# Sixth product of five w_out stages split into seven small products of the next w_in stage

## The chip, the cores and the metric

One core of one Trainium2 chip runs the kernel alone. The metric is device time in microseconds (us) of one execution; lower is better. The engines are TensorE (PE, matmuls), VectorE (DVE), ScalarE (ACT), GpSimd (POOL) and SyncE (SP); PSUM takes the results of PE, and DVE and ACT move them out ("evict" them).

## What is computed

Softmax attention over 8 batches, 12 heads, 448 positions and 64 dimensions a head, and then a two-layer network over the 3584 tokens:

```python
scores = (1 / sqrt(64)) * q @ k.transpose(0, 1, 3, 2)
attn = softmax(scores)
x = (attn @ v).transpose(0, 2, 1, 3).reshape(3584, 768)
h = x @ w_in                        # 768 x 2048
y = maximum(0.01 * h, h) @ w_out    # 2048 x 768
```

## The kernel before, in words

**Two matrix products, each by seven.** Both products of the network are done in bf16 by Winograd's form of Strassen's scheme: a 2 x 2 block product takes seven block products, with sums of blocks made by DVE beforehand (`x_mix`, `w_in_mix`, `h_mix`, `w_mix`) and sums of results made as they leave PSUM.

**Stages.** The tokens are cut at 0, 640, 1152, 1664, 2176, 2688, 3072 and 3584 into seven stages. From stage 1 on, the kernel is a sequence hidden(1), second(1), hidden(2), ..., second(6). `hidden(i)` (L525 to 605) makes the leaky-ReLU layer of stage i, `second(i)` (L1140 on) its outputs. Attention for later stages is done in between: "bursts" of scores and exponentials (L322, L331) inside second, and "rows" (the product of the exponentials and v, L343 and L350, with a reciprocal and a multiplication by DVE, L978 and L979), in both. Where bursts and rows go is settled while the program is built, by a small planner (`place`) that holds a model of when each engine and slot comes free. The finished x is transposed into `xT` by DMAs that SP issues (L276), q and k into `qkT` likewise (L285). POOL loads q, k and v and casts them.

**PSUM.** Two banks, `g0` and `g1`, and three slots, `sc0` to `sc2`, of two banks each (a tile of 128 x 2 x 512 fp32).

**hidden.** Two rounds r (0, 1) of seven steps; in each step, two chains each do one product of six matmuls (L548), 256 columns wide in a stage of 512 tokens. The chain "g" alternates between g0 and g1, the chain "sc" between the first banks of two slots (sc2 and sc1; `chains`, `b` and `a`). In round 0 each step does sc first, then g; in round 1 g first. What evicts a product, by step: 0, an ACT copy (L560); 1, a DVE add (L563); 2 and 3, ACT copies (L568, L572); 4 and 5, DVE adds (L575, L578); 6, an ACT Prelu straight from PSUM. Further Prelus (L537) turn the sums into h. Rows stand behind steps 1 and 3 of round 1 in hidden(2) to hidden(5); hidden(6) has none.

**second.** Two `block_pair`s (c = 0, 1), each with two blocks of 128 tokens and outputs `o1` and `o2`. `early()` and `late()` do six products of eight matmuls of 384 columns (L682) on g0 and g1 in turn: first and second into o1's left half, third into its right half (`keep` copies, `join` adds; L687, L693), fourth into o2's right half, fifth into o2's left half and added to its right, and the sixth, on top of the fourth's bank, into o1's right half, which is then stored.

**The seventh product, already split.** Its two parts (c = 0 and 1) are not done in second but in the next hidden, together: as one product of 256 tokens x 1024 by 1024 x 384 that is split once more by Winograd's form into seven runs of four matmuls of 192 columns. `deep(i)` (L621 to 660) does one run (L645) behind each step from step 1 of round 0 on, in the two banks of slot sc0; each run is added to o2 by DVE (L649). Its sums of h are made by `deep_sums` (L621) and one more (L651), those of the weights by `mix_deep`. In stage 6 it is done inside second.

Of the kernel before, what the change touches and what calls it, by code (L numbers as in the profile page):

```python
# [16 lines left out]
def kernel(  # L17
# [9 lines left out]
    nc = tc.nc  # L27
# [21 lines left out]
    w_pool = ctx.enter_context(tc.tile_pool(name="weights", bufs=1))  # L49
    ld_pool = ctx.enter_context(tc.tile_pool(name="ld", bufs=2))  # L50
    cast_pool = ctx.enter_context(tc.tile_pool(name="cast", bufs=1))
    v_pool = ctx.enter_context(tc.tile_pool(name="vones", bufs=1))
# [5 lines left out]
    h_pool = ctx.enter_context(tc.tile_pool(name="h", bufs=1))  # L58
    o_pool = ctx.enter_context(tc.tile_pool(name="o", bufs=3))
    c_pool = ctx.enter_context(tc.tile_pool(name="c", bufs=5))  # L60
# [41 lines left out]

    NX = 12 * P

    def place_of(t):
        return (t - cuts[5]) % NX

    OVER = max(-t % S for t in cuts if place_of(t) == 0)
    xT_flat = xT_pool.tile([P, KD * NX + OVER], BF16, name="xT")
# [6 lines left out]
    QH, QW = MH // 2, NW // 2  # L116
    deep_mix = w_pool.tile([P, 3, QH, QW], BF16)
    KEEP = 4
    h = h_pool.tile([P, MD, (KEEP + 1) * P], BF16, name="h")
# [15 lines left out]
    for t in (w_in_mix, w_mix):  # L135
        t = t.rearrange("p x k n -> p (x k n)")
        for j in range(9):
            rooms.append(t[:, ts(j, 4 * NSC * D)])
    for _ in range(3):
        rooms.append(o_pool.tile([P, DM], F32, name="o").bitcast(BF16)[:, :4 * NSC * D])  # L140
    for j in range(2):
# [4 lines left out]
    def room(x, new):  # L146

        n = P if x and new else SC
        if not rooms:
            return ld_pool.tile([n, 2, NSC, D], F32, name="f" + "qkv"[x])  # L150
        return rooms.pop(0)[:n].bitcast(F32).rearrange("p (h so d) -> p h so d", h=2, so=NSC)
# [295 lines left out]

    def mix_deep():

        t, (t2, t3, t4) = w_mix[:, 2], (deep_mix[:, x] for x in range(3))  # L450
        lo, hi, left, right = slice(0, QH), slice(QH, MH), slice(0, QW), slice(QW, NW)
        sub, add = nc.vector.tensor_sub, nc.vector.tensor_add
        for by, o, x, y in (
            (sub, t3, t[:, hi, right], t[:, lo, right]),
            (add, t2, t3, t[:, lo, left]),
            (sub, t4, t[:, hi, left], t2),
            (sub, t[:, lo, right], t[:, lo, right], t[:, lo, left]),
        ):
            by(o, x, y)
            yield  # L460
# [19 lines left out]
    def close_ring(i):  # L480

        if place_of(cuts[i]) == 0 and cuts[i] % S:
            for hp in range(KD):
                nc.vector.tensor_copy(xT[:, hp, :OVER], xT_flat[:, (hp + 1) * NX:(hp + 1) * NX + OVER])
                yield
# [37 lines left out]
    def hidden(i):  # L523
# [9 lines left out]
        del slots[1:]  # L533
        chains = [banks, [x[:, 0] for x in taken]]

        def act(m, cols, x):
# [4 lines left out]
        def group(chain, m):  # L541
            b, a = (x[:, :2 * nh] for x in chain)
            left, right = slice(0, nh), slice(nh, n)
# [24 lines left out]
            nc.scalar.copy(c12, b)  # L568
            yield
            product(a, w_in_sb[:, near, ch], xT[:, near, two], first=True)  # L570
            c22 = fresh()
# [13 lines left out]

        ready = []
        more = deep(i - 1) if i > 1 else None
        for r in range(2):
            ms = [4 * r, 4 * r + 2]
            todo = [group(chains[x], ms[x]) for x in range(2)]  # L590
            for step in range(7):
                for y in range(2):
                    x = y if r else 1 - y
                    yield
                    if r == 0 and step == 2 and y:
                        nc.vector.tensor_sub(t4, xT[:, far, one], t2)
                    next(todo[x])
                    if i > 1 and (r or step) and y == 1:
                        next(more, None)
                    if step == 2 and ready:  # L600
                        mix_h(i, ready.pop(0))
            for c in chains:
                c.reverse()
            ready += ms
# [5 lines left out]

    def deep_sums(i):

        one, two = (ts(x[1], P) for x in spots(i)[1])
        lo, hi = slice(MH, MH + QH), slice(MH + QH, MD)
        s3, s1 = h_mix[:, :QH, 0], h_mix[:, QH:, 0]
        for by, o, x, y in (
# [6 lines left out]

    def deep(i):

        one, two = (ts(x[1], P) for x in spots(i)[1])
        lo, hi = slice(MH, MH + QH), slice(MH + QH, MD)
        s3, s1 = h_mix[:, :QH, 0], h_mix[:, QH:, 0]
        t, (t2, t3, t4) = w_mix[:, 2], (deep_mix[:, x] for x in range(3))
        left, right = slice(0, QW), slice(QW, NW)  # L630
        o = [kept[i, c] for c in range(2)]
        end = i + 1 == NR
        taken = [slots.pop(0) for _ in range(2 if end else 1)]
        b, a = (x[:, 0, :QW] for x in taken) if end else (taken[0][:, x, :QW] for x in range(2))
        for ps, first, x, w, c, cols in (
            (b, True, h[:, lo, one], t[:, :QH, left], 0, left),
# [3 lines left out]
            (b, False, s3, t3, 1, right),  # L640
            (a, False, h[:, hi, one], t[:, QH:, right], 0, right),
            (b, False, h[:, hi, two], t4, 1, left),
        ):
            for m in range(QH):
                nc.tensor.matmul(ps, x[:, m], w[:, m], start=(first and m == 0), stop=(m == QH - 1), skip_group_check=True)  # L645
            if end and c and (ps is a or cols is left):
                nc.scalar.copy(o[c][:, cols], ps)
            else:
                nc.vector.tensor_add(o[c][:, cols], o[c][:, cols], ps)  # L649
            if ps is a and first and c == 0:  # L650
                nc.vector.tensor_sub(h[:, hi, one], h[:, hi, one], s1)  # L651
            if ps is a and not first:
                store(o[0], token(i, spots(i)[1][0][1]), slice(0, NW) if end else slice(0, DM))
            if w is t4:
                if not end:
                    store(o[1], token(i, spots(i)[1][1][1]))
                slots.extend(taken)
            yield

    def block_pair(i, c):  # L660
# [10 lines left out]
        else:  # L671
            o1, o2 = (o_pool.tile([P, DM], F32, name="o") for _ in range(2))
        kept[i, c] = o2
        b, a = banks
# [20 lines left out]
        def early():  # L695
# [19 lines left out]
            yield from product(a, h[:, lo, two], t1, first=True)  # L715
            keep(o2, right, a, calm)
            yield

        def late():
            yield from product(b, s3, t3)  # L720
            if i:
                keep(o2, left, b, calm)
            join(o2, right, b)
            if i + 1 == NR:
                store(o2, t0, right)
            yield
            yield from product(a, h[:, hi, one], w_out_sb[:, hi, right])
            join(o1, right, a)
# [26 lines left out]
        if last:  # L755
            more = deep(i)
            for x, _ in enumerate(early()):
                if x == 0:
                    next(parts[0])
                yield  # L760
                if x % 2:
                    next(more)
                    yield
            for _ in more:
                yield
            yield from closing()
            return
        if not c:
            parts[:] = [deep_sums(i)]
        for x, _ in enumerate(early()):  # L770
# [3 lines left out]
        for x, _ in enumerate(late()):  # L774
            if i and not c and (x == 4 or x == 6 and i + 1 == NR):
                next(parts[0])
            yield
        if i:
            return
        yield  # L780
# [155 lines left out]
    def advance(calm=True):  # L936
        have = list(to["load"])
        for x in range(3 if calm else 0):
            u = to["load"][x]
            if u < NU and u - 3 < (to["cast"], to["cast"], to["v"])[x] and u - 4 < min(to["load"]):  # L940
                load_soft(u, 2, (x,))
                to["load"][x] += 2
# [84 lines left out]
    def fetch(n=3):  # L1027
        if to["q"] == NPE:
            return
        for x, y in enumerate(("q", "cast", "v")):  # L1030
            u = to["load"][x]
            if n and u <= ahead and (u <= FAR or u - 3 < to[y]):
                load_soft(u, 2, (x,))
# [104 lines left out]
    def second(i):  # L1138
# [5 lines left out]
        for c in range(len(spots(i)[1])):  # L1144
            for x, _ in enumerate(block_pair(i, c)):
# [6 lines left out]
                left -= place(i, left if i or c or x > 1 else 0, calm=x not in ((1, 2, 3) if i == 5 else (1, 2)), keen=need[min(i + 2, NR)], cap=NU if all(summed) else need[i + 2])  # L1152
                if c or x < 20 or not 0 < i < NR - 2:
                    turn_next(i)
                if i == 0 and not c:
# [21 lines left out]

    ins, outs, deeps = mix_w_in(), mix_weights(), mix_deep()
    early = [1, 2, 4, 6, 7, 9, 11]
# [28 lines left out]
    for i in range(1, NR):  # L1208
        if i == 1:
            await_x(need[i + 1] - 1)  # L1210
        for step, _ in enumerate(hidden(i)):
# [3 lines left out]
            if step % 4 == 2 and rows_done < nxt and (step > 16 or i == 1):  # L1215
                rows()
            turn_next(i)
        model.update(now=0.0, act=2.3, free={id(x): 0.9 if cuts[i + 1] - cuts[i] == 4 * P and i + 1 < NR else 1.2 for x in slots}, ready={})
        second(i)
# [30 lines left out]
```

## Time and profile before

| | |
|---|---|
| Median of 3 runs | 377.83 us (377.81 to 378.04) |
| Profiled execution | 377.8 us, of which the span of the profile is 376.0 |
| Granted PE clock | 1.0 |
| PE busy | 368.8 us, 4008 matmul rows |
| DVE, ACT, POOL busy | 255.9, 259.9, 190.6 us |
| hidden(2), hidden(3), hidden(4) | 22.66, 22.64, 22.65 us |
| hidden(5) (384 tokens), hidden(6) | 18.17, 20.65 us |
| second(1) to second(4) | 25.4 us each |
| second(5) | 23.57 us |

A page of the profile gives busy time by engine, the chain of work that ended last, and groups of instructions by line. The timeline gives single rows: start in us from the span's start, length, engine, line, operation and tile, how many instructions it sums up, and in brackets how long the engine was idle before it and what released it. A stage begins where its first matmul begins.

### The profile page before, as it was taken

The page shows a single profiled execution, that of the slowest core. Times are in us where ns is not written, and L with a number is a line of the kernel's source. Part 1 is how long each engine was busy: PE and PEld are TensorE (multiplying, and loading weights), DVE is VectorE, ACT ScalarE, POOL GpSimd, SP SyncE. Part 2 cuts the span into 40 slices and gives each one's busy share as a digit, 9 for nine tenths or more (in the row PEclk, how much of TensorE's full clock was granted, in tenths as well). Part 3 has the DMA queues.
Part 4 walks back from the last instruction along what each step waited for, and adds up shares of the span by engine and source line. Part 5 has one row for each costly group of instructions (what it writes and reads, how often), then busy time and mean ns, then how long its engine had stood idle before and what let it go on. Part 6 is the DMA issues. An engine that isn't in the chain of part 4 may idle for free.

```text
span 376.0 us, 10120 instructions
## 1 busy us (share of the span) xinstructions
PE 368.8 (98%) x4008; PEld 265.3 (71%) x4008; DVE 255.9 (68%) x559; ACT 259.9 (69%) x399; POOL 190.6 (51%) x376
## 2 busy tenths in 40 slices
PE   7999999999999999999999999999999999999996
PEld 3665658756698566996569966699665995679765
DVE  4764868767666967676686665875747775685763
ACT  6998895866768785758766587666787668636721
POOL 8985871996269979634588335692346020000000
PEclk9999999999999999999999999999999999999999
DMA  9999999999499876963969648999445740321123
GB/s 155 200 203 207 175 203 202 166 165 168 92 186 150 113 149 89 204 154 55 162 120 150 138 65 80 166 145 180 63 66 108 131 110 0 80 57 45 41 65 105
DMA packets 99600, 48.08 MB, mean 128 GB/s; under 512 B 64608, under 2 KB 96352, under 8 KB 99552
## 3 DMA queue, kind: packets, MB, share of 16 engines
q0 software_dynamic: 39600, 22.47, 45.6%
q1 hardware_dynamic: 59504, 24.50, 32.5%
q8 instruction: 31, 0.51, 0.6%
q10 hardware_dynamic: 448, 0.47, 0.4%
q14 instruction: 17, 0.14, 0.1%
HBM read 45.61 MB, written 11.01 MB: 151 GB/s over the span
## 4 chain that ended last, share of the span: by engine, by line
PE 95%; DMA 2%; DVE 1%; POOL 1%; ACT 1%; issue 0%; POOLq 0%; ACTq 0%
PE g L682 30%; PE g L548 14%; PE sc L548 14%; PE sc L322 7%; PE sc L350 6%; PE g L424 4%; PE sc L319 4%; PE sc L645 4%; PE sc L362 3%; PE g L820 2%; PE sc L343 2%; DMA w_in_mix<-in_v_dram 2%; PE g L362 1%; PE g L301 1%; PE sc L424 1%; POOL w_in_mix L163 1%
## 5 line engine op out<-in xcount | busy, mean ns | idle before, releaser
L331 ACT ACTIVATE e<-sc 128x896 bf16<-128x896 f32 (+1 forms) x144 | 123.6, 921 | 29.9 <-PE sc L322 20.4
L682 PE MATMUL g<-w_out_sb,h 128*128 128x384 bf16 (+1 forms) x440 | 84.1, 325 | 0.0
L682 PEld LDWEIGHTS <-h 128*128 128x128 bf16 x592 | 54.4, 98 | 41.2 <-issue 11.0
L537 ACT ACTIVATE h<-c 128x512 bf16<-128x512 f32 (+1 forms) x72 | 43.1, 610 | 30.2 <-DVE c L563 12.4
L548 PEld LDWEIGHTS <-w_in_sb 128*128 128x128 bf16 x576 | 54.6, 98 | 5.7
L190 POOL COPY qkb<-fq 112x512 bf16<-112x512 bf16 x34 | 22.6, 666 | 43.8 <-DMA qkT<-qkb 34.7
L548 PEld LDWEIGHTS <-w_in_mix 128*128 128x128 bf16 x432 | 40.5, 98 | 3.7
L201 POOL COPY v<-fv 128x384 bf16<-128x384 bf16 x30 | 17.7, 591 | 42.7 <-PE sc L350 40.2
L687 DVE COPY o<-g 128x384 f32<-128x384 f32 x47 | 26.0, 553 | 13.2 <-PE g L682 13.0
L350 PE MATMUL sc<-v,e 128*128 128x65 bf16 x720 | 33.3, 193 | 0.0
L322 PE MATMUL sc<-qkT 64*128 64x448 bf16 (+1 forms) x210 | 32.8, 352 | 0.0
L978 DVE RECIPROCAL rec<-sc 112x8 f32<-112x8 f32 x42 | 8.7, 207 | 34.7 <-PE sc L350 19.4
L350 PEld LDWEIGHTS <-e 128*128 128x128 bf16 x720 | 31.1, 98 | 1.3
L979 DVE TENSOR_TENSOR x<-sc,rec 112x512 bf16<-112x512 f32 x42 | 29.0, 691 | 1.6 <-DVE rec L978 0.2
L548 PE MATMUL g<-xT,w_in_sb 128*128 128x256 bf16 (+1 forms) x216 | 28.5, 268 | 0.0
L548 PE MATMUL sc<-xT,w_in_sb 128*128 128x256 bf16 (+1 forms) x216 | 28.5, 268 | 0.0
L693 DVE TENSOR_TENSOR o<-o,g 128x384 f32<-128x384 f32 x39 | 21.4, 550 | 9.0 <-PE g L682 4.4
L343 PE MATMUL sc<-v,e 128*128 128x130 bf16 x120 | 26.5, 221 | 0.0
L649 DVE TENSOR_TENSOR o<-o,sc 128x192 f32<-128x192 f32 x39 | 13.7, 351 | 18.3 <-PE sc L645 18.3
L682 PE MATMUL g<-w_mix,h 128*128 128x384 bf16 x128 | 24.6, 326 | 0.0
L163 POOL DMA_DIRECT2D fv<-in_v_dram x32 | 20.1, 641 | 7.8 <-DMA fq<-in_q_dram 2.9
L682 PE MATMUL g<-w_mix,hmix 128*128 128x384 bf16 x112 | 21.7, 326 | 0.0
(149 smaller groups left out, 742.4 us busy)
## 6 DMA issues: line engine op xcount, KB each, us to landing
fq<-in_q_dram POOLq DMA_DIRECT2D x17, 224.0 KB, 6.1
w_out_sb<-in_moe_w_out_dram POOLq DMA_DIRECT2D x4, 768.0 KB, 13.2
out_dram<-o SPq DMA_DIRECT2D x7, 336.0 KB, 3.3
w_in_sb<-in_moe_w_in_dram POOLq DMA_DIRECT2D x2, 1152.0 KB, 13.6
out_dram<-o SPq DMA_DIRECT2D x7, 288.0 KB, 3.1
fk<-in_k_dram POOLq DMA_DIRECT2D x15, 128.0 KB, 6.0
fv<-in_v_dram POOLq DMA_DIRECT2D x15, 128.0 KB, 5.1
out_dram<-o SPq DMA_DIRECT2D x7, 240.0 KB, 3.1
```

The costliest lines, as they stand in the source:

```text
L163: nc.gpsimd.dma_start(out=t[p, :n, :, :so].rearrange("p u h so d -> p (u h) (so d)"), in_=(q, k, v)[x][b, hs, keys].rearrange("h (p so) d ...
L190: by(t[:SC, x].rearrange("p so h d -> p h so d"), f)
L322: nc.tensor.matmul(ps[:, j, :S].rearrange("p (so s) -> p so s", so=NSC), t[p, 1, c], t[p, 0, :, :SC], start=True, stop=True,)
L331: nc.scalar.activation(e[:, :, c, :], ps[:n, :, :S], AX.Exp, scale=scale)
L343: nc.tensor.matmul(ps, e[:, EM + qc * SC:EM + qc * SC + P], vt[:, 2 * KC:].rearrange("p j d -> p (j d)"), start=True, stop=False, skip_gro ...
L350: nc.tensor.matmul(ps[:, j * (D + 1):(j + 1) * (D + 1)], e[:, at:at + P], vt[:, j * KC + c], start=False, stop=(c == KC - 1), skip_group_c ...
L537: nc.scalar.activation(hs[:, m:m + 2, cols], x.rearrange("p (m t) -> p m t", m=2), AX.Prelu, alpha=0.01)
L548: nc.tensor.matmul(ps[:, j * nh:(j + 1) * nh], w[:, kk, ts(j, P)], x[:, kk], start=(first and j == 0 and kk == 0), stop=(kk == KH - 1), sk ...
L682: nc.tensor.matmul(ps[:, cols], x[:, m], w[:, m], start=(first and m == 0), stop=(m == MH - 1), skip_group_check=True,)
L687: by(o[:, at], ps[:, :NW])
L693: nc.vector.tensor_add(o[:, at], o[:, at], ps[:, :NW])
L979: nc.vector.tensor_mul(x, ps[:, :, :, :D], rec.to_broadcast([SC, 2, 2 * NP, D]))
```

## The change

For stages 1 to 5 (`twice(i)`), second no longer does the sixth product. `deep(i, side, b, a)` now does either split product: side 1 is the seventh ("more"), side 0 the sixth ("also"). In hidden(i + 1), runs of the sixth are issued behind the first product of the steps (0, 3), (0, 4), (0, 6), (1, 0), (1, 1), (1, 3) and (1, 4) (round, step). They take the two banks of sc1, one of the two slots of the sc chain; that chain, from step 3 of round 0 on, alternates between the two banks of sc2. The seventh keeps sc0.

With it come: the fourth product is joined to o1 as well at once, in `early()`; the copy of o2's left half goes to ACT in the second pair (`idle`); four weight sums for the sixth (`mix_deep(0)`, into `deep_mix6` and, in place, a quarter of `w_out_sb`), made in hidden(1); since stage 6 still does its sixth product whole, POOL reloads that quarter of w_out after hidden(6). The o pool has four buffers, v's loads a pool of their own with one buffer, and the ring `xT` nine blocks of 128 tokens where it had twelve, with more small copies where a stage wraps (`close_ring`).

The core of the diff:

```diff
-    NX = 12 * P
+    NX = 9 * P
...
+    deep_mix6 = w_pool.tile([P, 3, QH, QW], BF16)
...
+    def deep_w(side):
+        t, d = (w_mix[:, 2], deep_mix) if side else (w_out_sb[:, MH:, NW:], deep_mix6)
+        return t, [d[:, x] for x in range(3)]
+    def twice(i):
+        return 0 < i < NR - 1
...
         chains = [banks, [x[:, 0] for x in taken]]
+        more, also, over = (iter(()) for _ in range(3))
+        if i > 1:
+            third = slots[0]
+            more = deep(i - 1, 1, *(third[:, x, :QW] for x in range(2)))
+            also = deep(i - 1, 0, *(taken[1][:, x, :QW] for x in range(2)))
+            chains[1].append(taken[0][:, 1])
+        else:
+            over = mix_deep(0)
...
-            b, a = (x[:, :2 * nh] for x in chain)
+            b, a, *then = (x[:, :2 * nh] for x in chain)
...
             nc.scalar.copy(c12, b)
             yield
+            for a in then:
+                pass
             product(a, w_in_sb[:, near, ch], xT[:, near, two], first=True)
...
+                    if i > 1 and (r, step, y) == (0, 1, 1):
+                        for _ in deep_sums(i - 1, 0):
+                            pass
+                    if not y and (r, step) in ((0, 3), (0, 4), (0, 6), (1, 0), (1, 1), (1, 3), (1, 4)):
+                        next(also, None)
...
             for c in chains:
-                c.reverse()
+                if len(c) == 3:
+                    c[:] = [c[2], c[0]]
+                else:
+                    c.reverse()
...
+            at = slice(cols.start + (0 if side else NW), cols.stop + (0 if side else NW))
+            for y in (c, 0) if ps is a and c and not side else (c,):
+                if end and c and (ps is a or cols is left):
+                    nc.scalar.copy(o[c][:, at], ps)
+                else:
+                    nc.vector.tensor_add(o[y][:, at], o[y][:, at], ps)
...
             keep(o2, right, a, calm)
+            if twice(i):
+                join(o1, right, a)
             yield
...
             if i:
-                keep(o2, left, b, calm)
+                keep(o2, left, b, idle if c and twice(i) else calm)
             join(o2, right, b)
...
+            if twice(i):
+                return
             yield from product(a, h[:, hi, one], w_out_sb[:, hi, right])
             join(o1, right, a)
             store(o1, token(i, x1))
...
+        if i + 1 == NR:
+            raw_q = (slice(None), slice(MH, MH + QH), slice(NW + QW, DM))
+            nc.gpsimd.dma_start(out=w_out_sb[raw_q], in_=w_out_v[raw_q])
```

## The prediction on record

> **What bounds the kernel now.** I read the page first: busy shares, then the chain that ended last.
>
> ```profile
> PE 368.8 (98%) x4008; PEld 265.3 (71%) x4008; DVE 255.9 (68%) x559; ACT 259.9 (69%) x399; POOL 190.6 (51%) x376
> PE 95%; DMA 2%; DVE 1%; POOL 1%; ACT 1%; issue 0%; POOLq 0%; ACTq 0%
> ```
>
> TensorE (PE) is busy 98% of the span, and 95% of the chain that sets the end is PE. The table of stretches says the same by stage: in hidden(2) (147.58 to 170.24 us) PE is busy 22.66 of 22.66 us, at a granted clock of 1.00, and so in all stages but the last. So a stage is as long as its matmuls, and two things alone move the time: matmul time taken out or put in, and waits that PE does not have today.
>
> Then the timeline, for the price of a matmul: the end of second(1) and the start of hidden(2), PE rows (start, length, then engine, line and tile; a row's length contains the drain of its last matmul, so prices are taken from start to start).
>
> ```profile
> 146.28 1.46 PE L682 MATMUL g<-w_out_sb,h 128*128 128x384 bf16 x8
> 147.58 0.82 PE L548 MATMUL sc<-xT,w_in_sb 128*128 128x256 bf16 x6
> ...
> 149.54 0.82 PE L548 MATMUL g<-xT,w_in_sb 128*128 128x256 bf16 x6
> ...
> 150.20 0.49 PE L645 MATMUL sc<-w_mix,h 128*128 128x192 bf16 x4
> ...
> 150.53 0.82 PE L548 MATMUL sc<-x_mix,w_in_mix 128*128 128x256 bf16 x6
> ```
>
> Eight 384-column matmuls take 147.58 - 146.28 = 1.30 us; six of 256 columns 150.20 - 149.54 = 0.66; four of 192 columns 150.53 - 150.20 = 0.33 (four such runs follow each other at 0.328).
>
> Last, how long a PSUM result takes to be evicted, since the change gives one chain of hidden less PSUM. VectorE (DVE) and ScalarE (ACT) rows of hidden(2):
>
> ```profile
> 149.81 0.69 DVE L563 TENSOR_TENSOR c<-c,sc 128x512 f32<-128x512 f32 x1 [0.62 <-PE sc L548]
> ...
> 163.34 0.82 PE L548 MATMUL sc<-x_mix,w_in_mix 128*128 128x256 bf16 x6
> 163.99 0.82 PE L548 MATMUL g<-xT,w_in_sb 128*128 128x256 bf16 x6
> ...
> 164.07 0.63 ACT L537 ACTIVATE h<-c 128x512 bf16<-128x512 f32 x1
> 164.60 0.58 ACT L568 COPY c<-sc 128x512 f32<-128x512 f32 x1
> ```
>
> The first: DVE was idle and took the sc product that PE left at 149.54 (PE's next row starts there) 0.27 us later, for 0.69 us. With 0.06 from a DVE end to the PE row that waited for it (15.59 to 15.65, qkT at the start of the run) a DVE eviction is 0.27 + 0.69 + 0.06 = **1.02 us** after PE finishes. An ACT copy that finds ACT free takes 0.20 (151.18 to 151.38) + 0.59 + 0.05 = **0.84**. The last two rows: the sc product that ended at 163.99 was copied only from 164.60 to 165.18, since a Prelu stood ahead on ACT; that eviction took **1.24** with its return. None of these costs anything today, because each sc product lands in the slot that the product before it did not use.
>
> **The change, part by part.**
>
> *Matmuls.* In stages 1 to 5, two pairs each lose the 8 matmuls of the sixth product: 16 x 0.1625 = 2.60 us. The next hidden gains 7 runs of 4 matmuls: 7 x 0.328 = 2.30. Net -0.30 a stage, -1.5 us over five, all on PE and so all on the path.
>
> *PSUM.* This is where I see the price. The seven new runs need a slot. They take sc1, one of the two that hidden's sc chain alternated between; the seventh product keeps sc0. From step 3 of round 0 on, the sc chain therefore alternates between the two banks of one slot, sc2. In the kernel as built, dependences go by slot: each sc product from there on waits for the eviction of the sc product just before it, though that lies in the other bank. (In the kernel before, the second run of the seventh product, L645, already waits so for the L649 add of the first.) The cover is what PE has between two sc products: the g product (0.66), each deep run between (0.33), attention rows (1.02 in the row spacing 161.68 to 162.68). Step by step, for hidden(2) to (5):
> - round 0, steps 3, 4, 5: cover 0.98, 1.31, 1.31 against 0.84 (ACT), 0.84 (ACT), 1.02 (DVE): nothing.
> - round 0, step 6: 0.98 against 1.02: 0.04.
> - round 1, steps 1, 2, 4: cover 1.31, 1.67 and 2.0 (rows): nothing.
> - round 1, step 3: 0.98 (g and one run) against the queued copy's 1.24: 0.26; nothing if ACT is free.
> - round 1, step 5: only a g product, 0.66, against 1.02 for step 4's L575 add: 0.36. The add for g goes first on DVE; adds follow each other at 0.60 (167.95 to 168.55), so it may be 0.43.
> - round 1, step 6: 0.66 against 1.02 again: 0.36.
>
> Queued behind the waiting matmul is everything on PE, since PE works in order; DVE, ACT and the next second() wait for PE. So these go on the path whole.
>
> *Start of hidden.* The second run of the seventh product waits, as it does now, for the add of the first. Today that add ends at 151.42 and the run starts at 151.84: 0.36 to spare after 0.06 of return. The change loads DVE ahead of it: second() is 2.60 shorter but its last exps stay as long; `keep(o2, left)` goes to ACT behind them; the join of o2's other half reads the same bank and so follows that copy. Today ACT ends the last exp 1.34 before hidden starts (146.24 to 147.58); with a run of 8 less (1.30) it would end at about hidden's start, the copy 0.84 to 1.33 after it, the join (0.55) and the x sums (0.3 each) after that. I get the first run's add 0.86 later than today, the stall 0.86 - 0.36 = 0.5. Bounds: 0 and 0.5; I take 0.45, since each link is a row of today's trace.
>
> Sum of waits for one hidden: 0.45 + 0.04 + 0.26 + 0.40 + 0.36 = 1.5. hidden(5) has 192-column products (0.49 each; its add takes 0.55), cover and eviction shrink alike. hidden(6) has no rows: step 2 of round 1 loses cover (0.66 against 1.02: 0.36), and its start has a shorter queue (0.3): again 1.5. Five stages: **+7.5 us**.
>
> *Elsewhere.* Seven more adds of 192 columns (0.35) and four h sums (0.42) put about 4 us on DVE in a hidden where it is busy 15.7 of 22.7; they go where PE runs deep runs, and the adds above are priced with that order. At nothing I cost: the join of o1 (moved, not added); four `mix_deep(0)` sums in hidden(1) and twelve more ring copies in the second() before stages 2, 4 and 6 (0.3 to 0.5 each; second() leaves DVE 22 to 36% idle, by the stretches); the stores of o1 (SP, one hidden later; the qkT transposes behind them on SP are needed 5 us later or more); v loads in one buffer (the v casts that PE's rows need are done four rows, about 15 us, ahead); the raw quarter of w_out reloaded by POOL after hidden(6): 196 KB, issued when the sixth new run is done, needed about 10 us later; 224 KB loads land in 6.1 us by the page's DMA rows, so 4 us to spare, and if that cover is gone the stage waits up to 3 (the 768 KB load's 13.2 us). The xT transposes of a stage's last rows land 2.3 to 4.3 us from issue, and second() now ends 2.60 earlier: 0 to 0.3 us in a stage, taken as 0. Bursts move against DVE's x: 0 to 0.1 a stage, taken as 0.
>
> *Sum.* -1.5 + 7.5 = +6.0; I take off 0.3 because the step 3 and step 6 terms are partly nothing when ACT is early: **+5.7 us**. The profiled execution took 377.8 us (span 376.0 and 1.8 around it), the median of the runs is 377.83, so the two agree and the forecast is 377.8 + 5.7 = **383.5 us**.
>
> **Rivals.**
>
> *A. No new waits: faster.* If the two banks of a slot were free of each other, only the product two steps back would have to be evicted, more than 2 us earlier, and all terms but the one at hidden's start vanish: 377.8 - 1.5 = 376.3 (376.8 with a few tenths a stage left). It decides at round 1, step 5: an eviction under 0.66 us ends the stall, and the shortest in the trace is 0.84. For it: the trace of before shows no PE wait of this kind, as the one such pair (L645) has 0.36 to spare. Against: the waits as built. The Trainium skill (PSUM — Partial Sum Buffer, section "PSUM bank collisions raise a hardware error") asks for guards by bank and quadrant; a program so guarded would have no wait between the two banks, and the time would be A's 376.3. No run here shows that, and the waits of this kernel are coarser. Chance 0.12.
>
> *B. Only the two bare gaps.* The stalls at steps 5 and 6 of round 1 (0.36 + 0.40) are certain if waits go by slot; the queue effects (start of hidden, step 3) may be hidden, as ACT's order shifts once PE stalls. Then 5 x 0.76 + 0.36 = 4.2, less 1.5: 380.5. Chance 0.24 (379.3 to 381.5).
>
> *C. More than this.* DVE, at (15.7 + 4)/24 = 82% in hidden, falls behind after the first stall, or xT lands late: 0.5 a stage more, 386 and above. Chance 0.08.
>
> *Forecast*, waits as listed, 381.5 to 386: chance 0.53. The remaining 0.03 is small waits that eat the gain, about 377.8.
>
> **How the numbers follow.** Range 379.3 to 387.0: it holds forecast and B whole and the lower half of C (0.53 + 0.24 + 0.04 = 0.81); A is left out. Differences under 0.2% (0.75 us) are about what cannot be told from no change here. Faster: A, 0.12. Same: 0.03. Slower: the rest, 0.85.
>
> **What would show it.** PE in the changed trace should have idle time in front of sc rows of the product line (L548, now L578) at steps 5 and 6 of round 1, some 0.4 us each, released by DVE's add of the step before; a like gap before the second run of the seventh product, released by DVE; PE matmul time over the run should be 1.5 us less. second() of stages 1 to 5 should be 2.6 us shorter and hidden(2) to (6) about 3.8 longer (2.30 + 1.5). Wrong it would be if those rows follow each other without a gap (A), if the gap at hidden's start is missing (B), or if the wait in front of PE is released by a DMA or POOL.

## The result and the profile after

The changed kernel takes **390.2 us** (median of 6 runs, 389.64 to 391.70) where the kernel before takes 378.02 (6 runs): a ratio of 1.033, 95% interval 1.0309 to 1.0351, or 12.2 us more. The forecast was slower by 5.7 us, in a range up to 387.0. The sign was right, the size forecast was half of what came. The profiled execution took 389.64 us, with a span of 387.9 (before: 377.8 and 376.0).

The page of the changed kernel, the busy shares and the chain:

```profile
PE 372.2 (96%) x4068; PEld 269.3 (69%) x4068; DVE 273.5 (71%) x630; ACT 262.0 (68%) x404; POOL 190.5 (49%) x377
...
PE 79%; DVE 8%; DMA 5%; ACT 3%; issue 3%; POOL 1%; DVEq 0%; ACTq 0%; POOLq 0%
```

PE's share of the chain fell from 95% to 79%: DVE, DMA and ACT now set pieces of the end. The waits of PE, longest sums first (what PE waited to do, for what; us in total, times, longest):

```profile
PE sc L578 <- DMA xT<-x: 4.2, 2, 3.2
...
PE sc L578 <- DVE c L607: 1.2, 5, 0.4
...
PE sc L697 <- DVE o L703: 0.6, 3, 0.2
PE g L578 <- DVE o L746: 0.3, 1, 0.3
...
PE sc L578 <- DVE c L593: 0.2, 1, 0.2
```

The rows for DVE are waits of the kind that was forecast; the fourth (the second g product of hidden(5)) was not on the list. The first row was forecast at nothing. (These times start where PE could have gone on; the gap in the timeline, start to start less the price of the matmuls, is about 0.17 us longer each, and gaps are used below.)

By stage, start to start from the PE rows of the timelines: second(1) to (5) went from 125.28 to 112.75 us, -12.53 (forecast: 5 x 2.60 = -13.0). hidden(2) to (6) went from 106.79 to 130.47, +23.68: 11.48 for the seven runs of five stages (5 x 7 x 0.328, as forecast), and **12.2 us of waits** where 7.5 were forecast. The start (0.41) and second(6) (0.27) make up the rest of the 11.8 us by which the span grew.

**Two kinds of wait.** hidden(2) shows the kind that was forecast. PE rows of its round 1, steps 4 to 6, and the DVE rows that they wait for:

```profile
168.41 0.82 PE L578 MATMUL sc<-x_mix,w_in_mix 128*128 128x256 bf16 x6
169.07 0.82 PE L578 MATMUL g<-xT,w_in_mix 128*128 128x256 bf16 x6
170.08 0.81 PE L578 MATMUL sc<-xT,w_in_mix 128*128 128x256 bf16 x6 [0.19 <-DVE c L607]
170.73 0.82 PE L578 MATMUL g<-x_mix,w_in_sb 128*128 128x256 bf16 x6
171.67 0.82 PE L578 MATMUL sc<-x_mix,w_in_sb 128*128 128x256 bf16 x6
```

```profile
169.34 0.69 DVE L607 TENSOR_TENSOR c<-c,sc 128x512 f32<-128x512 f32 x1
169.94 0.68 DVE L610 TENSOR_TENSOR c<-c,g 128x512 f32<-128x512 f32 x1
170.93 0.69 DVE L610 TENSOR_TENSOR c<-c,sc 128x512 f32<-128x512 f32 x1 [0.31 <-PE sc L578]
```

The sc product of 168.41 ends for PE at 169.07; DVE adds it from 169.34 to 170.03, and the next sc product starts at 170.08, though a g product alone would have let it start at 169.72. The gap is 0.35, the next one (170.73 + 0.66 to 171.67) 0.28.

hidden(4) shows the other kind. PE rows, then the chain of work there (start, length, what), then the POOL rows:

```profile
246.41 0.38 PE L578 MATMUL sc<-xT,w_in_sb 128*128 128x256 bf16 x2
249.99 0.60 PE L578 MATMUL sc<-xT,w_in_sb 128*128 128x256 bf16 x4 [3.19 <-DMA xT<-x]
```

```profile
241.86 0.70 DVE x L1042
242.56 0.02 issue
242.57 7.37 DMA xT<-x
249.94 0.04 issue
249.99 0.60 PE sc L578 x4
```

```profile
241.35 1.23 POOL L175 DMA_DIRECT2D fv<-in_v_dram  x2
242.56 0.73 POOL L175 DMA_DIRECT2D fq<-in_q_dram  x1
243.25 1.26 POOL L175 DMA_DIRECT2D fk<-in_k_dram  x2
```

The last x of stage 4 is done at 242.56 and its transpose is issued at once, but lands 7.37 us later; PE stands still in the second sc product of hidden. POOL issued the next loads of v from 241.35 on, and q and k right behind, so 672 KB of loads were in front of the transpose or beside it; those of v were issued 1.2 us ahead of it. In the kernel before, POOL reached the like loads at 247.58, 3.8 us into hidden(4):

```profile
247.58 1.24 POOL L163 DMA_DIRECT2D fv<-in_v_dram  x2
248.79 0.73 POOL L163 DMA_DIRECT2D fq<-in_q_dram  x1
249.49 1.26 POOL L163 DMA_DIRECT2D fk<-in_k_dram  x2
```

### The profile page after: what moved, and what is told of

The parts are those of the page before. It is cut to its first block, busy times and chain, and to the rows that moved or that the text cites. A ratio compares the mean times of both kernels' runs of the same rounds, so it can differ in the third digit from the quotient of the medians.

```text
span 387.9 us, 10326 instructions
## 1 busy us (share of the span) xinstructions
PE 372.2 (96%) x4068; PEld 269.3 (69%) x4068; DVE 273.5 (71%) x630; ACT 262.0 (68%) x404; POOL 190.5 (49%) x377
## 4 chain that ended last, share of the span: by engine, by line
PE 79%; DVE 8%; DMA 5%; ACT 3%; issue 3%; POOL 1%; DVEq 0%; ACTq 0%; POOLq 0%
PE g L735 23%; PE sc L578 11%; PE g L578 9%; PE sc L334 6%; PE sc L362 6%; PE sc L697 6%; PE g L436 4%; PE sc L331 4%; DMA xT<-x 3%; PE sc L374 3%; PE g L883 2%; PE sc L355 2%; DMA w_in_mix<-in_v_dram 2%; DVE c L607 2%; PE g L374 1%
## 5 line engine op out<-in xcount | busy, mean ns | idle before, releaser
L735 PEld LDWEIGHTS <-h 128*128 128x128 bf16 x512 | 46.7, 98 | 35.9 <-issue 11.0
L735 PE MATMUL g<-w_out_sb,h 128*128 128x384 bf16 (+1 forms) x360 | 68.4, 325 | 0.0
L578 PEld LDWEIGHTS <-w_in_sb 128*128 128x128 bf16 x576 | 54.5, 98 | 12.8 <-issue 7.4
L202 POOL COPY qkb<-fq 112x512 bf16<-112x512 bf16 x34 | 24.3, 716 | 55.3 <-DMA qkT<-qkb 41.5
L213 POOL COPY v<-fv 128x384 bf16<-128x384 bf16 x30 | 16.6, 555 | 41.9 <-PE sc L362 26.7
L703 DVE TENSOR_TENSOR o<-o,sc 128x192 f32<-128x192 f32 x79 | 26.9, 348 | 10.2 <-PE sc L697 10.1
L740 DVE COPY o<-g 128x384 f32<-128x384 f32 x42 | 23.2, 553 | 13.1 <-PE g L735 11.2
L374 PEld LDWEIGHTS <-e 112*128 112x128 bf16 x432 | 20.1, 98 | 2.2 <-issue 0.8
```

Of the source, the lines that this page charges most:

```text
L202: by(t[:SC, x].rearrange("p so h d -> p h so d"), f)
L374: nc.tensor.matmul(ps[:, qc, :], t[:SC, at:at + P], vt[:, c], start=(c == 0), stop=(c == NSC - 1),)
L578: nc.tensor.matmul(ps[:, j * nh:(j + 1) * nh], w[:, kk, ts(j, P)], x[:, kk], start=(first and j == 0 and kk == 0), stop=(kk == KH - 1), sk ...
L703: nc.vector.tensor_add(o[y][:, at], o[y][:, at], ps)
L735: nc.tensor.matmul(ps[:, cols], x[:, m], w[:, m], start=(first and m == 0), stop=(m == MH - 1), skip_group_check=True,)
```

## The experiments

Two theories stood at the start. W: the sc chain waits by slot, as forecast. L: POOL's loads, moved ahead of the transposes, make xT late. Rivals: S, xT is late because second() ends 2.6 us sooner after the last x, whatever POOL does; D, the waits in hidden are VectorE's lack of room and not the slots.

### e1: POOL waits for xT

```diff
-        if i == 1:
+        if i + 1 < NR:
             await_x(need[i + 1] - 1)
```

> The changed kernel with one edit: ahead of each of hidden(1) to hidden(5), not of hidden(1) alone, POOL waits until the xT of that stage's last row has landed, so its next loads of q, k and v are issued behind that transpose. Theory L (loads first in the DMA engines make xT late): PE's waits for xT at the start of hidden(3) and (4), 4.2 us in the changed kernel's trace, go, and waits of about 0.36 us for the seventh product's second run come back in their place; 390.2 becomes about 386.5. Rival S (xT is late because second() ends 2.6 us sooner after the last row): the waits stay, within 1 us of 390.2. Rival P (POOL late then hurts its casts, and bursts wait for qkT): above 390.2.

Measured: **384.75 us** (ratio to before 1.0175, 1.0146 to 1.0204), 5.4 less than the changed kernel. PE waits for xT no more. POOL waits in its place: the transpose ahead of hidden(4) is issued at 241.15, has landed 2.5 us later at the most, by 243.65, and only then come the loads. The rows of POOL, the first with its wait:

```profile
243.65 0.18 POOL L1268 COPY word<-xT 128x2 bf16<-128x2 bf16 x1 [3.66 <-DMA xT<-x]
244.11 1.23 POOL L175 DMA_DIRECT2D fv<-in_v_dram  x2 [0.27 <-issue]
```

L stands; it gave more than was expected, and late casts cost nothing (rival P): second(1) to (5) sum to 112.75 us here too. What is left is the forecast's own list, without the disturbance: hidden(3) is 26.27 us, 22.66 + 2.30 + 1.3. Its gaps against the forecast, in us: second run of the seventh product 0.33 (0.45), round 0 step 6 0.05 (0.04), round 1 step 3 0.26 (0.26), step 5 0.35 (0.40), step 6 0.28 (0.36). Over the five hiddens, 19.46 - 11.48 = 8.0 us (7.5). That sum is nearer than its parts: hidden(2) to (4) have 1.3 us of waits each, hidden(6) 1.7 and hidden(5) 2.35, where 1.5 each was forecast. In hidden(5) the gap at step 5 is 0.56 (0.40): DVE is behind with a row's x there and comes to the sc product's add only 0.45 us after PE is done (312.80 to 313.25). Two more gaps stand near its start (0.47 and 0.24).

Of the 5.4 us, the traces show 4.2 in the five hiddens (130.47 against 126.25), and 0.6 at the start and in second(6), where PE waits for no xT; the rest lies in executions that have no trace.

### e3, e10, e11: which part of the change makes xT late

The root of POOL's new order is in the diff's rule for the one v buffer: v's loads are held until the last one is cast, and loads of q and k may not run four or more ahead of v's. So the next loads of v, q and k, which POOL had reached only in hidden behind its casts (247.58 above), stand at the end of second(), ahead of those casts (241.35 above). e3 is the kernel before with that rule alone; e10 the kernel before without the sixth product of stages 1 to 5 (left out, so a part of the output is missing); e11 has both.

```diff
-            if u < NU and u - 3 < (to["cast"], to["cast"], to["v"])[x] and u - 4 < min(to["load"]):
+            if u < NU and u - (3 if x < 2 or u <= HY else 1) < (to["cast"], to["cast"], to["v"])[x] and u - 4 < min(to["load"]):
```

> The kernel before with one rule of the change alone: a load of v is issued only when the one before it is cast, as the single v buffer asks; nothing else, no product is moved and no buffer taken away. By it POOL's order at the start of each hidden becomes that of the changed kernel (loads of v, q, k, then the casts of q and k, which had stood ahead). Theory L in its strong form (this rule alone brings the late xT): PE waits for xT in one or more of hidden(2) to (4), 379 to 382. Rival S: the last transposes are issued 4.8 us before hidden here (2.5 in the changed kernel), so the lead covers it: 377.8 to 378.3.

> The kernel before with the sixth product of stages 1 to 5 left out (not done anywhere, so a part of the output is missing) and nothing else changed: second() ends 2.6 us sooner after the last row, as in the changed kernel, while POOL keeps its old rule for loads of v. 378.0 - 5 x 2.60 = 365.0 if nothing waits. Theory L2 (late xT needs both: the shorter second and the new order of POOL's loads): PE's waits for xT stay under 1 us, 365 to 366.3. Rival S (the shorter second alone makes xT late): 367.5 to 369.5, with PE waiting for xT by 3 us or more.

> The same with the sixth product left out, and the rule for loads of v of the change (as in e3, where it cost nothing by itself). Theory L2: PE waits for xT as in the changed kernel, some 4 us, 368.5 to 370.5. If it is within 1 us of the run beside it, the order of the loads isn't the cause, and e1 gained by something else.

Measured: e3 378.06 us (ratio 1.000, 0.9987 to 1.0013), e10 366.16 (0.9690, 0.9676 to 0.9705), e11 368.86 (0.9745, 0.9711 to 0.9778). POOL's rows in e3 at the end of second(3), which have the changed kernel's order; PE's wait for xT in e10; the same in e11:

```profile
240.31 1.23 POOL L163 DMA_DIRECT2D fv<-in_v_dram  x2
241.52 0.73 POOL L163 DMA_DIRECT2D fq<-in_q_dram  x1
242.21 1.26 POOL L163 DMA_DIRECT2D fk<-in_k_dram  x2
```

```profile
PE sc L548 <- DMA xT<-x: 0.2, 1, 0.2
```

```profile
PE sc L548 <- DMA xT<-x: 2.5, 2, 2.0
```

So it takes both. The rule alone costs nothing: in e3 the last transpose is issued 4.8 us before hidden(4) starts (239.14 to 243.95), 1.2 us ahead of the loads, and lands in 2.3 us. The shorter second() alone costs little. Together they cost 2.7 us by the medians, and the transpose then stands behind the first load of v (188.06 against 187.60 ahead of hidden(3), where it takes 6.2 us). That is less than the 5.4 of e1; what else of the change adds to the late xT is not shown. S falls as a cause by itself.

A late xT can also cost more than the wait. In e11's trace PE waits 2.01 us in hidden(3), and from 195.0 to 198.4, soon after it has gone on, its granted clock is 0.51, which by that figure costs another 1.7 us. The trace of e2 (below) has such a stretch at 0.50, over 3 us long, after each of its two longer waits for xT (2.26 and 2.37 us), and none after the one of 1.12. But the changed kernel's trace has none after 3.19 us, so a long wait does not bring it each time. e11's runs lie between 366.91 and 370.22.

e10 tells one thing more. Leaving the product out gives 11.8 us, not 13.0: second(1) to (5) are 12.8 shorter, and the hiddens 1.2 longer with waits of their own. The seven runs cost 11.48. So even if the seven runs had brought no wait of their own, the change would have been worth some 0.3 us, not the 1.5 of the forecast.

### e2 and e4: the sixth product in both slots

The sc chain keeps its two slots; each run of the sixth takes the second bank of the slot that the sc product just before did not use. e4 has e1's edit as well.

```diff
-            also = deep(i - 1, 0, *(taken[1][:, x, :QW] for x in range(2)))
-            chains[1].append(taken[0][:, 1])
+            also = deep(i - 1, 0, *(taken[1 - x][:, 1, :QW] for x in range(2)))
...
-                    if not y and (r, step) in ((0, 3), (0, 4), (0, 6), (1, 0), (1, 1), (1, 3), (1, 4)):
+                    if x and (r, step) in ((0, 2), (0, 3), (0, 5), (0, 6), (1, 1), (1, 2), (1, 3)):
```

> The changed kernel with the slots shared otherwise: the sc chain keeps its two slots for the whole of hidden, and the runs of the sixth product take the second banks of these two slots, each run in the slot that the sc product just before it did not use, at steps (0,2), (0,3), (0,5), (0,6), (1,1), (1,2), (1,3). The work is the same. Theory W (waits go by slot, on the eviction of the sc product just before): the gaps of 0.26, 0.35 and 0.28 us before the sc products of steps 3, 5 and 6 of round 1 go, and 0.36 at step 2 in hidden(6): 5 x 0.89 + 0.36 = 4.8 us, 390.2 becomes about 385.4. Rival D (VectorE is behind in hidden, whatever the slots): the gaps stay or move, 389 to 391.

> The edits of the two runs above together, in the changed kernel: POOL waits for xT, and the runs of the sixth product lie in both slots. If W and L hold and add, 390.2 - 3.7 - 4.8 = 381.7. If the two hide each other, 384 or more. What is left above 377.8 - 1.5 = 376.3 would be the waits at hidden's start.

Measured: 389.2 us (ratio 1.0303, 1.0256 to 1.0349) and 384.65 (1.0173, 1.0146 to 1.0200). e2 can't be told from the changed kernel (388.32 to 391.90 against 389.64 to 391.70), nor e4 from e1. In hidden(2) to (4) of e4 the waits by slot were gone, and another stood there. PE's waits in e4:

```profile
PE sc L577 <- DVE o L702: 4.8, 6, 0.9
```

L702 (L703 in the changed kernel) is the add of a deep run. The first run now stood at step 2 of round 0, and the sc product of step 3 had to wait for its add, while DVE was still behind from the end of second(): in hidden(2) DVE's rows follow each other without a pause from 146.31 on, and the add comes at 150.69, 1.65 us after PE is done with the run. So D holds at hidden's start, and W in round 1.

### e5, e6, e7: VectorE's backlog, and both slots one step later

e5 is e1 with the last copy of o2's left half on DVE again; e6 is e1 with the runs in both slots, the first at step 3; e7 has both.

```diff
-                keep(o2, left, b, idle if c and twice(i) else calm)
+                keep(o2, left, b, calm)
```

```diff
-                    if not y and (r, step) in ((0, 3), (0, 4), (0, 6), (1, 0), (1, 1), (1, 3), (1, 4)):
+                    if x and (r, step) in ((0, 3), (0, 4), (0, 5), (0, 6), (1, 1), (1, 2), (1, 3)):
...
-            todo.insert(1, todo.pop(3))
+            todo.insert(0, todo.pop(3))
```

> The kernel in which POOL waits for xT (e1: 384.75 us), with one more edit: in second(1) to (5) the last copy of o2's left half is VectorE's again, not ScalarE's behind the last exps. Theory Q (the wait of 0.34 us ahead of the seventh product's second run, and the 0.3 us ahead of the second g product in hidden(5), come from VectorE's join that waits for that ScalarE copy): both go, 5 x 0.34 + 0.3 = 2.0 us, 382.8. Rival: VectorE is as late with its own copy (0.5 us more of work there): within 0.5 of 384.75.

> e1 with the sixth product's runs in both slots, as in e4, but the first of them one step later (steps (0,3) to (0,6), (1,1), (1,2), (1,3), the first two runs exchanged). In e4 the waits by slot at round 1 went and a new one of 0.9 us stood at step 3 of round 0, where VectorE, behind at hidden's start, had not yet done the first run's add. Theory W: with that run after VectorE has caught up, the 0.26 + 0.35 + 0.28 a stage and 0.36 in hidden(6) are gone and nothing comes instead: 384.75 - 4.8 = 380.0. Rival D (VectorE's backlog costs as much wherever the runs stand): 383.5 or more.

> e5 and e6 together. If W and Q both hold and add: 384.75 - 4.8 - 2.0 = 378.0, the time of the kernel before; the last 1.5 us to 376.3 would be what stays of small waits.

Measured: e5 383.1 us (ratio 1.0144, 1.0126 to 1.0161), e6 384.27 (1.0175, 1.0154 to 1.0196), e7 381.64 (1.0099, 1.0078 to 1.0120). Q holds in hidden(2) to (4): the gap before the seventh product's second run is gone there, as is the one of 0.47 in hidden(5), and e5 is 1.65 less than e1. In hidden(5) and (6) that second run still waits (0.28 and 0.37); in e10, which never had ScalarE's copy, it waits there too (0.19 and 0.37), so there the shorter second() is enough. In e6 the gaps of round 1 in hidden(3) are gone too (0.26, 0.35 and 0.28 in e1), but 0.54 us stands before step 4 of round 0: the run before it has two adds (o1 and o2), and the sc product waits for both. In e7 that is 0.44; its hidden(3) is 25.41 us, 22.66 + 2.30 + 0.45. W and D are both true, each of its place: a wait removed by another slot came back as a wait for DVE.

### e8 and e9: two more orders

In e8 (e1 with the runs at (0,3), (0,4), (0,6), (1,0), (1,3), (1,5), (1,6)) runs read sums and values of h that hidden has by then replaced, and in e9 (e7 with the two-add run at (1,0), and the sums of h one step later) one run reads h that hidden has overwritten; so each computes terms from other data, and in e8 PE also waits for the engines that wrote them.

> e1 with the runs of the sixth product at other steps and nothing else: those of (1,1) and (1,4) now stand at (1,5) and (1,6), between the products whose gaps were bare, (1,3) as before. The waits by slot stay in the program; only the cover changes, from 0.66 to 0.98 against 1.02. Theory W: the gaps of 0.35 and 0.28 go and leave 0.04 each; 5 x 0.55 = 2.8 us, 382.0. Rival (those gaps are VectorE's throughput, not the distance between two products): 384 to 385.

> e7 (381.64 us) with the sixth product's runs once more in another order, all in both slots: the run with two VectorE adds goes from step 3 of round 0 to step 0 of round 1, where the sc product before is evicted by ScalarE, and a run with one add takes step 3; the three sums of h for these runs are made one step later, behind the seventh product's second add. Theory W: the gap of 0.44 to 0.54 us ahead of step 4 in e7 shrinks to about 0.1 and the 0.36 at hidden's start in hidden(6) by half: 381.64 - 5 x 0.4 - 0.3 = 379.3. If all waits in hidden were gone it would be 376.3, below the kernel before. Rival D (VectorE has no room for the 8 adds and 4 sums, and any order gives the same): 381.2 or more.

Measured: 386.91 us (ratio 1.0242, 1.0221 to 1.0262) and 382.96 (1.0125, 1.0103 to 1.0147). In e8's hidden(3) the gap at step 5 of round 1 did shrink, 0.35 to 0.08, as W has it for more cover; but the run at step 6 waited 0.84 for ScalarE's h. In e9 the wait that was to shrink to 0.1 stayed, 0.49 ahead of step 4 in hidden(3), and the run with two adds brought one of 0.29 to its new place, as D has it. For the total both are inconclusive. They show why the runs stood where they did: hidden overwrites the data that they read, from the end of round 0 on.

## Why the prediction was right or wrong

- **What bounds the kernel**: right. No wait was absorbed: e1's waits in hidden sum to 8.0 us, its matmuls save 12.53 - 11.48 = 1.05, and its time is above the kernel before by 6.8.
- **Matmuls, -1.5 us**: the pace was right (2.30 added a stage), the saving too big. second() gave 12.53 us, not 13.0.
- **PSUM, waits by slot**: right in mechanism, and in size in hidden(2) to (4), gap by gap (e1). In hidden(5) cover and eviction did not "shrink alike": 0.56 at step 5. That the sum came out at 8.0 for 7.5 is in part luck, as too much for three stages offset too little for the last two. The bank-wise guards of the Trainium skill (PSUM — Partial Sum Buffer, section "PSUM bank collisions raise a hardware error") were cited for rival A; no run here shows a program so guarded, and A is out.
- **Start of hidden, 0.45**: right in cause for hidden(2) to (4) (e5), where it measured 0.33 to 0.34. In hidden(5) and (6) it measured 0.37, and e5 leaves most of it. In hidden(5) the same late join also held the second g product, 0.47 us, which was not listed.
- **Elsewhere: the step that failed.** The prediction put "v loads in one buffer" at nothing, and the xT transposes at "0 to 0.3 us in a stage, taken as 0". Both terms were looked at one by one: whether casts of v come in time (they do), and what transposes had taken so far (2.3 to 4.3 us). What was not asked is what POOL does instead. The one-buffer rule moved the loads to the end of second(), and there the transpose took 7.37 us, with its lead over hidden cut from 4.8 to 2.5. The trace of before held a sign of it: in second(3) two transposes that were not a stage's last, issued at 227.31 and 231.10, took 5.5 and 6.7 us to land, with loads of q and k issued from 227.79 on. That term is 390.2 - 384.75 = 5.4 us by the medians. It came with the sign that the prediction had named for itself, a wait of PE released by a DMA. The rest of the miss, 384.75 - 383.5 = 1.25, is 0.5 in the waits, 0.5 in second(), and the 0.3 that had been taken off.
- **Rivals**: C named a late xT, at 0.5 us a stage and a chance of 0.08; the place was right and the price a half of it. B is out, as the waits at the start of hidden and at step 3 are there.

No version here that computes the whole output is faster than the kernel before. The best with the sixth product moved, e7, is 3.8 us above it.

## What to carry to other kernels

When a change alters the rule by which an engine issues transfers, follow that engine's queue past the next deadline of every other transfer, and ask which of them now lies in front. A shorter stage shortens the lead of whatever must land at its end, so a cover that was ample before is to be measured again against the new start. Where accumulators are shared, count the time between two products that use the same one against the eviction: 0.66 us of cover against 1.02 was worth 0.28 to 0.36 us each time in hidden(2) to (4), and taking the wait out only paid where the engine that evicts had room just then (e7, not e4).

## What the hardware showed that was not expected

A transpose of x that lands within 2.5 us of its issue with no load in flight (e1) took 7.37 us beside 672 KB of loads that another engine issued from 1.2 us before to 1.9 us after it. The Trainium skill (DMA: Bandwidth & Descriptors, section "Issuing engines are not separate DMA queues") says that transfers issued by different engines run on the same 16 DMA engines and interleave; the traces are in line with it, with 7.37 us beside the loads and 2.5 without. The times also lie further apart with xT late, 2.1 us in the changed kernel (389.64 to 391.70) and 3.3 in e11, against 1.2 with POOL made to wait (384.35 to 385.52). That this is the landing's doing is not shown: the stretches of half clock (above) move the time too, and 13 runs of the kernel before lie 2.3 us apart (377.46 to 379.78).
